# A gated mix of a Fourier layer and a SwiGLU: the gate/up stage written out in one order, and the stream's loads moved to ScalarE

## The chip, the cores and the metric

The kernel runs on one core of a Trainium2 chip. A core has TensorE (PE, matrix products, with PEld for its weight loads), VectorE (DVE), ScalarE (ACT), GpSimd (POOL) and SyncE (SP). Each takes its own instructions strictly in order; they meet only at semaphores. SP, ACT and POOL can also start transfers (DMAs); all transfers of the core share 16 DMA engines. The metric is device time in microseconds (us), lower is better. The kernel before took 740.35 us, the median of three runs (739.05 to 740.51).

## The reference

Sequence length S = 2048, width D = 512, hidden width F = 1376, all in float32. Cut to its core:

```python
a = einsum("bsd,ed->bse", x, dft_hid_re)
b = einsum("bsd,ed->bse", x, dft_hid_im)
y = einsum("ts,bse->bte", dft_seq_re, a) - einsum("ts,bse->bte", dft_seq_im, b)
h = silu(x @ w1) * (x @ w3)
out = h @ w2
g = sigmoid((x * gate_w).sum(-1, keepdims=True))
return g * y + (1 - g) * out
```

## The kernel before, in words

**Precision.** Each float32 operand is split into a high part (a float32r copy made by ScalarE, `nc.scalar.activation` with Copy, L110) and a low part (the difference, `nc.vector.tensor_sub`, L111). A product is three matmuls: high by high, high by low, low by high (`mm3`, L113). Everything TensorE reads has therefore passed through ScalarE and VectorE; the helper `split` does both halves at once.

**Fewer products.** Each 2x2 block product is done with seven products of sums of blocks instead of eight products (a Strassen-Winograd scheme). The sums of blocks, called T1 to T4 on the streamed side, are made on VectorE, the results are collected from TensorE's eight accumulation banks by ScalarE and VectorE.

**Gate/up stage.** Work is cut into 22 items, `ITEMS` (L163): a chunk c of 128 hidden columns times a half g of the sequence. Items 0 to 8 are chunks 0 to 8 for half 0, items 9 to 12 chunks 9 and 10 for both halves, items 13 to 21 chunks 0 to 8 for half 1, whose weights' sums are read back from DRAM (`load_wb`, L207). Item 0 is done with eight plain products. Every other item is `gate_up(n)` (L310), which calls `second(n, ...)` (L285): products into bank X (index 4), Z (5), then `first1(n+3)` (first product of the item three ahead, its own X bank), X (3), Z (2), then `first2(n+3)` (a Y bank), X (6). The document calls them X44, Z55, X33, Z26 and X62. Each accumulates into a bank which ScalarE or VectorE must have read before the next product goes in: u2 is copied from X (L292), u4 from Z (L294), u4 is added to (L297), u2 is added to and multiplied (L299, L300), and the Silu of X (L304) and a multiplication (L305) finish the item; GpSimd stores its result (`store_h`, L278). The Silu is what frees bank X for `first1` of the item after.

**What else is done during the items.** The weights: loads by SP (`load_w`), split of the three plain blocks (`prep_wa`) and sums and split of the other four (`prep_wb`, which also stores them through GpSimd for later). The operand of half 1, XO: four loads, four sums, seven splits at items 3 to 9 (L433 to L439). Four of the six parts of w2, at items 9 to 12 (`prep_w2`, L447): five sums and four splits, and two stores by GpSimd. The sequence-side input x, eight parts A1, seven of them at items 13 to 19 (`make_a`, L461): three sums into a second buffer and two splits each. These are hung into the dictionary `extra` by item and run at the end of `gate_up`.

**Order.** `manual_schedule` for PE and SP (L566) says that these two engines take their instructions as written in the gate/up stage. The order on VectorE, ScalarE and GpSimd there is chosen by a planner from its own estimates of durations; it moves later work between an item's steps. After the gate/up stage all engines are in written order (L575).

**Buffers.** `wide` (L98) takes a 4 KB-per-partition buffer from the list F4, four in the gate/up stage and nine more after it, in memory that the gate/up pools give up. `parts` (L101) takes one for a split pair from ZO, two in the gate/up stage and four after it. Both lists are first in, first out, in program order; an instruction that writes a reused buffer waits for its last reader or store.

**The stream.** 182 steps (`STEPS`, L489) in eight blocks: four "F" blocks (sequence DFT, 28 steps of 12 matmuls each), two "H" (hidden result by w2) and two "Y" (hidden DFT). A block runs through the seven products P1 to P4 of `CHAIN`, each in NQ steps. Step m's `step(m)` does the matmuls, then calls `advance(m)` (L561): `load_c(m + 8)` starts all loads that are due, `sum_c(m + 4)` makes a sum, `split_c(m + 3)` splits the operand for three steps ahead. After the first `split_c` of a B22 block, GpSimd starts an accumulating load that adds B12 into the same buffer (L551): that is operand T3. At the last step of a product its banks are read (ScalarE copies, VectorE adds) and, for four of them, scaled and stored by SP (`spill`, L644). Other work of that time hangs in `todo` by step: the second part of x (`make_a2`, steps 1, 3, ...), the gates (`gates`, a Sigmoid, step 2), the remaining w2 and DFT parts (`late_*`), and the loads of the next block's weights (`load_forms`, SP).

**The seam** between the stages: after item 21, `split_c(0)` and `split_c(1)`, the gate/up pools are closed and the new ones opened in their place, the last part of A1 is made, `advance(-1)` follows, and then the steps begin.

Of the kernel before, what the change touches and what calls it, by code (L numbers as in the profile page):

```python
# [26 lines left out]
K = 9  # L27
XO_AT = 3
W2_AT = (9, 10, 11, 12)
A1_AT = (13, 14, 15, 16, 17, 18, 19)  # L30


@with_exitstack
def fnet_swiglu_gate_kernel(
# [69 lines left out]
    def free(*tiles):  # L104
        for t in tiles:
            _, places, at = HELD.pop(id(t))
            places.append(at)

    def split(hi, lo, src):
        nc.scalar.activation(hi, src, AF.Copy)  # L110
        nc.vector.tensor_sub(lo, src, hi.bitcast(F32))  # L111

# [31 lines left out]
    def splits1(m, t1):  # L144
        split(flat(t1[:, 0, 1:4]), flat(t1[:, 1, 1:4]), m[:, :768])

    def forms1(r, m, t1):
        sums1(r, m, t1)
        splits1(m, t1)

# [37 lines left out]
    def sum_xo(g, k, t):  # L188
        ST[g, k] = t
        nc.vector.tensor_sub(t, *(ST[g, v] for v in SUMS[k]))  # L190

    def split_xo(g, k):
        o = XO[g][:, :, OPS.index(k)]
        split(flat_x(o[:, 0]), flat_x(o[:, 1]), ST[g, k])

# [11 lines left out]
    def load_wb(w):  # L207
        WB[w] = wbp.tile([P, 2, 4, 256], F32R, tag="wb", name=f"wb{w}")
        nc.sync.dma_start(WB[w].bitcast(F32), wbsp[SETS[w]])

    def prep_wa(w, lo=0, hi=3):

        if lo == 0:
            WA[w] = wap.tile([P, 2, 3, 256], F32R, tag="wa", name=f"wa{w}")
        t = WA[w]
        split(t[:, 0, lo:hi].rearrange("p a n -> p (a n)"),
              t[:, 1, lo:hi].rearrange("p a n -> p (a n)"),
              WS[w][:, lo:hi].rearrange("p a n -> p (a n)"))

    def prep_wb(w):  # L220

        r = WS.pop(w)
        u = wup.tile([P, 4, 256], F32, tag="wu", name=f"wu{w}")
# [4 lines left out]
        t = WB[w] = wbp.tile([P, 2, 4, 256], F32R, tag="wb", name=f"wb{w}")  # L228
        split(t[:, 0].rearrange("p a n -> p (a n)"), t[:, 1].rearrange("p a n -> p (a n)"),
              u.rearrange("p a n -> p (a n)"))  # L230
        if w < K:
            nc.gpsimd.dma_start(wbsp[w], t.bitcast(F32))

# [29 lines left out]
    def put_score(n, j, gate):  # L263


        c, g = ITEMS[n]
        if c < NC - 1:
            return
        if j == 0:
            SC[g] = wide(f"sc{g}")  # L270
        t = SC[g].rearrange("p (b n) -> p b n", b=2)
        nc.scalar.activation(t[F % P :, j], gate[F % P :], AF.Copy)
        if j == 1:
            nc.gpsimd.dma_start(gs[2 * g : 2 * g + 2].rearrange("b o n -> o b n"),
                                t[F % P : F % P + 1])
            extra.setdefault(n + 1, []).append(lambda: free(SC[g]))

# [6 lines left out]

    def second(n, between):  # L285
# [4 lines left out]
        u4 = u4p.tile([P, 512], F32, tag="u4", name=f"u4_{n}")  # L290
        prod(x, n, 4, 4, False, True)
        nc.scalar.activation(u2, x, AF.Copy)  # L292
        prod(z, n, 5, 5, True, True)
        nc.scalar.activation(u4, z, AF.Copy)  # L294
        between[0]()
# [5 lines left out]
        between[1]()  # L301
        prod(x, n, 6, 2, False, True)
        put_score(n, 1, x)
        nc.scalar.activation(g1, x, AF.Silu)  # L304
        nc.vector.tensor_mul(g1, g1, u4)  # L305
        store_h(n, h)

    extra = {}

    def gate_up(n):  # L310
        last = NI - 1

        def b0():
            w = WSET[min(n + LOOK, last)] + 1
            if w < len(SETS) and w not in WA and w not in WS:
                load_w(w, 0, 3 if back(w) else 4)
            if n < last and WSET[n + 1] not in WB:
                prep_wb(WSET[n + 1])
            if n + LOOK <= last:
                first1(n + LOOK)  # L320

        def b1():
            if n + LOOK < last and WSET[n + LOOK + 1] not in WA:
                prep_wa(WSET[n + LOOK + 1])
            if n + LOOK <= last:
                first2(n + LOOK)

        if n < last and WSET[n + 1] not in WB and back(WSET[n + 1]):
            load_wb(WSET[n + 1])
        if n + LOOK <= last and WSET[n + LOOK] not in WA:  # L330
            prep_wa(WSET[n + LOOK])
        second(n, (b0, b1))
        for f in extra.get(n, ()):
            f()

# [90 lines left out]
    WS.pop(0)  # L426
    load_w(4)


    def xo_sum(k, b):  # L430
        return lambda: (sum_xo(1, k, ST[1, b]), split_xo(1, k))

    extra[XO_AT - 2] = [lambda k=k: load_xo(1, k) for k in ("B11", "B21", "B12", "B22")]  # L433
    for n, f in enumerate((lambda: split_xo(1, "B11"), lambda: split_xo(1, "B21"),
                           xo_sum("T1", "B11"), xo_sum("T2", "B11"), xo_sum("T3", "B12"),
                           xo_sum("T4", "B21"), lambda: split_xo(1, "B22"))):
        extra[XO_AT + n] = [f]
    for n, k in enumerate((("B12",), ("B11", "B21"), ("B22",))):
        extra[XO_AT + 4 + n].append(lambda k=k: free(*(ST[1, b] for b in k)))  # L439

    W2R = {}

    def load_w2(p):
        W2R[p] = wide(f"w2r{p}")
        nc.sync.dma_start(W2R[p], w2[p])

    def prep_w2(p):  # L447
        r, m, t1, t2 = W2R.pop(p), wide(f"w2m{p}"), parts(f"w2a{p}"), parts(f"w2b{p}")
        forms1(r, m, t1)
        nc.gpsimd.dma_start(w2sp[0][p], t1.bitcast(F32))  # L450
        forms2(r, t2[:, :, :3])
        nc.gpsimd.dma_start(w2sp[1][p], t2[:, :, :3].bitcast(F32))
        free(r, m, t1, t2)

# [5 lines left out]

    def make_a(p, pl=None):  # L461
        A1.append((pl or a1).tile([P, 2, 4, 256], F32R, tag=f"a1_{p}", name=f"a1_{p}"))
        r, m = XR.pop(p), wide(f"xm{p}")
        forms1(r, m, A1[p])
        free(r, m)

    for p, n in enumerate(W2_AT):
        extra.setdefault(n - 1, []).append(lambda p=p: load_w2(p))
        extra.setdefault(n, []).append(lambda p=p: prep_w2(p))
    for p, n in enumerate(A1_AT):  # L470
        extra.setdefault(n - 1, []).append(lambda p=p: load_a(p))
        extra.setdefault(n, []).insert(0, lambda p=p: make_a(p))
    extra.setdefault(NI - 2, []).append(lambda: load_a(NG - 1))
    extra[NI - 1] = [lambda: load_c(2)]

# [78 lines left out]
    def load_c(m):  # L554
        while LOADS and LOADS[0][0] <= m and F4:
            _, blk, k, q = LOADS.pop(0)
            r = RAW[blk, k, q] = wide(f"{k}_{blk}_{q}")
            n = cols(blk, q, k)
            nc.sync.dma_start(r[:, :n], block(blk, "B12" if k == "T3" else k, q)[:, :n])

# [16 lines left out]
    split_c(1)  # L577
    close(*gate_pools)
# [6 lines left out]
    ZO[:0] = [(zo_b, f"zo_{k}") for k in range(2, 4)]  # L585
    make_a(NG - 1, a1b)
    advance(-1)
# [110 lines left out]
    def step(m):  # L698
# [17 lines left out]
        ni = cols(blk, q, form) // 512  # L716
        for r in range(2):
            sl = slice(r * P, (r + 1) * P)
            for n, zn in steps:
                for i in range(ni):  # L720
                    w = ws[2 * n + i]
                    b = slice(i * 512, (i + 1) * 512)
                    mm3(ps[r], w[:, 0, FORM[k], sl], w[:, 1, FORM[k], sl], zn[:, 0, b], zn[:, 1, b],
                        own and n == 0 and i == 0, n == NQ[blk] - 1 and i == ni - 1, not own)
# [136 lines left out]
```

## Time and profile before

One execution was profiled.

| what | value |
|---|---|
| median of three runs | 740.35 us |
| the profiled execution, its own time | 739.09 us |
| its span, first to last instruction | 737.2 us |
| TensorE clock granted, mean | 0.998 |
| ScalarE busy, VectorE busy | 366.2 us (50%), 575.8 us (78%) |
| bytes moved | 186.16 MB, mean 253 GB/s |
| gate/up items 1 to 21 on TensorE | from about 24 to 231 us |
| stream on TensorE | from about 226 to 733 us |

Busy time counts an instruction from its start to its end. Neighbouring instructions of one engine overlap a little, so the sum of durations is more than the busy time. The idle time in brackets behind a row is that of the engine just before it, with the instruction that ended it. A row "L110" or "L111" is the helper `split`, so its tiles tell what is split: zo is an operand of the stream, B a raw block for it, w2a and w2b the splits of w2 with w2r as raw data, xr and xs parts of x, wa and wb weights, xo the operand of the gate/up stage, h, u, s results.

### The profile page before, as it was taken

Reading aid. Unit: us, or ns where it says so; the run is one execution under the profiler, and the core shown is the slowest. Engines: PE = TensorE matmul, PEld = TensorE weight load, DVE = VectorE, ACT = ScalarE, POOL = GpSimd, SP = SyncE. Lnnn points to the kernel's source line nnn. Section 1 sums busy time; section 2 is a strip of 40 time slices with the busy share of each in tenths; the row PEclk is TensorE's granted clock in tenths of the full one; section 3 lists DMA queues with packets and bytes.
Section 4 is the critical chain, followed back from the end, with each engine's and each line's share of the span. In section 5 each row is a group of like instructions: output and inputs, shape, how many; then the busy total and the mean of one; then the engine's idle time right before and its main releaser. Section 6 shows DMA issues by size and latency. Waiting matters only on the chain.

```text
span 737.2 us, 8514 instructions
## 1 busy us (share of the span) xinstructions
PE 714.3 (97%) x3089; PEld 578.1 (78%) x3089; DVE 575.8 (78%) x717; ACT 366.2 (50%) x485; POOL 50.6 (7%) x74
## 2 busy tenths in 40 slices
PE   9999998899999899999999999999999999999997
PEld 6788876688887687888888887887778888887786
DVE  6999885757656887887798759985878596693996
ACT  6775553555433664445454445354535445444361
POOL 0111111110000010001000010001001001000000
PEclk9999999999999999999999999999999999999999
DMA  6665676667769757775967495829999689698862
GB/s 256 231 262 221 261 273 221 247 207 265 266 226 368 286 145 217 280 269 178 271 230 269 140 284 196 338 71 264 353 418 401 149 324 316 162 370 267 282 220 98
DMA packets 49625, 186.16 MB, mean 253 GB/s; under 512 B 5168, under 2 KB 5296, under 8 KB 44976
## 3 DMA queue, kind: packets, MB, share of 16 engines
q1 hardware_dynamic: 39728, 143.15, 53.6%
q0 software_dynamic: 9568, 41.96, 18.8%
q8 instruction: 24, 0.39, 0.2%
q10 hardware_dynamic: 288, 0.52, 0.2%
q14 instruction: 17, 0.14, 0.1%
HBM read 128.45 MB, written 57.16 MB: 252 GB/s over the span
## 4 chain that ended last, share of the span: by engine, by line
PE 45%; DMA 20%; issue 14%; DVE 13%; ACT 6%; SPq 1%; POOL 0%; ACTq 0%; POOLq 0%; DVEq 0%
PE P L115 24%; PE X L115 11%; DMA B<-cc 8%; PE Z L115 5%; DVE zo L111 5%; PE Y L115 3%; ACT zo L110 3%; DMA B<-zsp 3%; DMA B<-hsp 2%; DMA w2sp<-w2b 2%; DVE B L535 2%; DMA xs<-xn 1%; DMA dsp<-late 1%; PE C L115 1%; DMA p5g<-gs 1%
## 5 line engine op out<-in xcount | busy, mean ns | idle before, releaser
L115 PE MATMUL P<-zo,a 128*128 128x512 f32 x1344 | 311.4, 392 | 8.1 <-DVE zo L111 6.1
L115 PEld LDWEIGHTS P<-zo,a 128*128 128x128 f32 x1344 | 252.4, 189 | 66.9 <-DVE zo L111 10.9
L110 ACT ACTIVATE zo<-B 128x1024 fp32r<-128x1024 f32 (+1 forms) x182 | 187.6, 1044 | 214.9 <-DVE B L535 67.4
L111 DVE TENSOR_TENSOR zo<-B,zo 128x1024 fp32r<-128x1024 f32 (+1 forms) x182 | 216.9, 1204 | 88.5 <-ACT zo L110 87.7
L115 PE MATMUL P<-zo,H 128*128 128x512 f32 x468 | 106.5, 389 | 0.2 <-DVE zo L111 0.2
L115 PEld LDWEIGHTS P<-zo,H 128*128 128x128 f32 x468 | 87.8, 188 | 18.8 <-DVE zo L111 0.6
L115 PE MATMUL X<-xo,wb 128*128 128x512 f32 x378 | 93.6, 391 | 3.9 <-ACT h L292 3.9
L535 DVE TENSOR_TENSOR B<-B,B 128x1024 f32<-128x1024 f32 (+1 forms) x78 | 92.9, 1191 | 2.2 <-DMA B<-hsp 2.0
L115 PEld LDWEIGHTS X<-xo,wb 128*128 128x128 f32 x378 | 70.3, 188 | 21.2 <-ACT h L292 6.3
L115 PE MATMUL P<-zo,Y 128*128 128x512 f32 x336 | 77.5, 391 | 1.1 <-DVE zo L111 0.8
L115 PEld LDWEIGHTS P<-zo,Y 128*128 128x128 f32 x336 | 62.8, 188 | 15.6 <-DVE zo L111 2.7
L115 PE MATMUL X<-xo,wa 128*128 128x512 f32 x126 | 32.9, 392 | 4.3 <-ACT h L304 3.5
L115 PE MATMUL Y<-xo,wa 128*128 128x512 f32 x126 | 32.1, 389 | 0.0
L115 PE MATMUL Z<-xo,wb 128*128 128x512 f32 x126 | 32.1, 389 | 0.0
L115 PE MATMUL Z<-xo,wa 128*128 128x512 f32 x126 | 32.0, 389 | 0.0
L115 PEld LDWEIGHTS X<-xo,wa 128*128 128x128 f32 x126 | 23.4, 188 | 10.4 <-ACT h L304 4.4
L115 PEld LDWEIGHTS Z<-xo,wa 128*128 128x128 f32 x126 | 23.7, 188 | 5.0
L115 PEld LDWEIGHTS Z<-xo,wb 128*128 128x128 f32 x126 | 23.6, 188 | 4.9
L115 PEld LDWEIGHTS Y<-xo,wa 128*128 128x128 f32 x126 | 23.6, 188 | 4.9
L297 DVE TENSOR_TENSOR u<-u,X 128x512 f32<-128x512 f32 x21 | 14.4, 685 | 16.6 <-PE X L115 16.5
L551 POOL DMA_DIRECT2D B<-cc x16 | 13.7, 857 | 197.5 <-DVE zo L111 182.8
L110 ACT ACTIVATE wa<-ws 128x768 fp32r<-128x768 f32 (+2 forms) x21 | 17.0, 811 | 20.0 <-PE Z L115 11.7
(107 smaller groups left out, 530.8 us busy)
## 6 DMA issues: line engine op xcount, KB each, us to landing
B<-cc SPq DMA_DIRECT2D x64, 512.0 KB, 6.7
hsp<-h POOLq DMA_DIRECT2D x22, 512.0 KB, 5.2
B<-hsp SPq DMA_DIRECT2D x20, 512.0 KB, 9.6
wbsp<-wb POOLq DMA_DIRECT2D x8, 1024.0 KB, 5.1
wb<-wbsp SPq DMA_DIRECT2D x8, 1024.0 KB, 5.1
B<-cc POOLq DMA_DIRECT2D x16, 512.0 KB, 10.6
B<-zsp SPq DMA_DIRECT2D x16, 512.0 KB, 7.4
H<-w2sp SPq DMA_DIRECT2D x6, 1024.0 KB, 10.6
```

What stands on the lines that cost most here:

```text
L110: nc.scalar.activation(hi, src, AF.Copy)
L111: nc.vector.tensor_sub(lo, src, hi.bitcast(F32))
L115: nc.tensor.matmul(ps, u, v, start=first and n == 0, stop=last and n == 2, skip_group_check=chain)
L297: nc.vector.tensor_add(u4, u4, x)
L535: nc.vector.tensor_add(t, t, RAW[blk, b, q][:, :n])
L551: nc.gpsimd.dma_start(src, block(blk, "B12", q), accum_op=ALU.add)
```

## The change

Seven things are changed, all in the order or the place of work; the products are the same.

- `split` is divided into `high` (ScalarE) and `low` (VectorE), so that the two halves can stand at different places. `prep_wb` is likewise divided into its sums, its high and its low part.
- `gate_up` is written out as one order for all engines: between the seven products of an item stand the reads of its banks, the next weights' work, and three lists of later stages' work, `early` (after X44), `mid` (after X33) and `at_end`. `manual_schedule` now covers all engines from item 1 to the end.
- XO's splits, w2's parts and A1's parts go into these lists in pieces: sums in `early` of item n, high in `mid` of item n, low in `early` of item n+1. w2 is at items 9, 11, 13, 15 (was 9 to 12), A1 at 12, 14, 16 to 20 (was 13 to 19).
- A1 is made in place: three sums that overwrite the raw buffer and one split of all four blocks, in another order of columns (`FORMS`), instead of a second buffer and two splits.
- The two halves' scores share one buffer.
- The first two loads of the stream's first block come at the ends of items 19 and 20 (before, the first three at the end of item 21), and their splits in item 21. The split of weight set 4 stands before item 1.
- The stream's operand loads due from step 0 on are issued by ScalarE, ahead of the split in the same `advance`.

The diff, cut to its core:

```diff
-W2_AT = (9, 10, 11, 12)
-A1_AT = (13, 14, 15, 16, 17, 18, 19)
+W2_AT = (9, 11, 13, 15)
+A1_AT = (12, 14, 16, 17, 18, 19, 20)
...
+    def high(hi, src):
+        nc.scalar.activation(hi, src, AF.Copy)
+
+    def low(hi, lo, src):
+        nc.vector.tensor_sub(lo, src, hi.bitcast(F32))
...
+    def sums1_here(r):
+        a21, a11, a12, a22 = (r[:, i * 256 : (i + 1) * 256] for i in range(4))
+        nc.vector.tensor_sub(a22, a22, a21)
+        for d, v, w in ((a21, a22, a11), (a12, a12, a21)):
+            nc.vector.scalar_tensor_tensor(d, v, -1.0, w, op0=ALU.mult, op1=ALU.subtract)
...
     def gate_up(n):
...
         prod(x, n, 4, 4, False, True)
         nc.scalar.activation(u2, x, AF.Copy)
+        run(early, n)
         prod(z, n, 5, 5, True, True)
         nc.scalar.activation(u4, z, AF.Copy)
+        if nw is not None:
+            sums_wb(nw)
+        if n + LOOK <= last:
+            first1(n + LOOK)
+        if nw is not None:
+            high_wb(nw)
         prod(x, n, 3, 3, False, True)
         nc.vector.tensor_add(u4, u4, x)
+        if nw is not None:
+            low_wb(nw)
+        run(mid, n)
         prod(z, n, 2, 6, False, True)
         nc.vector.tensor_add(u2, u2, z)
         nc.vector.tensor_mul(u2, s1, u2)
+        if wa is not None:
+            WA[wa] = wap.tile([P, 2, 3, 256], F32R, tag="wa", name=f"wa{wa}")
+            parts_a = wa_parts(wa, 0, 3)
+            high(parts_a[0], parts_a[2])
+        if n + LOOK <= last:
+            first2(n + LOOK)
+        if wa is not None:
+            low(*parts_a)
         prod(x, n, 6, 2, False, True)
         put_score(n, 1, x)
         nc.scalar.activation(g1, x, AF.Silu)
         nc.vector.tensor_mul(g1, g1, u4)
         store_h(n, h)
+        run(at_end, n)
...
+    prep_wa(4)
...
+    for n, (k, b) in enumerate((("B11", ""), ("B21", ""), ("T1", "B11"), ("T2", "B11"),
+                                ("T3", "B12"), ("T4", "B21"), ("B22", ""))):
+        if b:
+            do(early, n + 2, lambda k=k, b=b: sum_xo(1, k, ST[1, b]))
+        do(mid, n + 2, lambda k=k: high(*xo_parts(1, k)[::2]))
+        do(early, n + 3, lambda k=k: low(*xo_parts(1, k)))
...
+        if n in W2_AT:
+            p = W2_AT.index(n)
+            do(at_end, n - 1, load_w2, p)
+            do(early, n, sums_w2, p)
+            do(mid, n, high_w2, p)
+            do(early, n + 1, low_w2, p)
+        if n in A1_AT:
+            p = A1_AT.index(n)
+            do(at_end, n - 1, load_a, p)
+            do(early, n, lambda p=p: sums1_here(XR[p]))
+            do(mid, n, high_a, p)
+            do(early, n + 1, low_a, p)
+    do(at_end, NI - 3, lambda: load_c(0))
+    do(at_end, NI - 2, load_a, NG - 1)
+    do(at_end, NI - 2, lambda: load_c(1))
+    do(early, NI - 1, lambda: sums1_here(XR[NG - 1]))
+    do(mid, NI - 1, lambda: split_c(0))
+    do(at_end, NI - 1, lambda: split_c(1))
...
+    FORMS = {"F": FORM | {"P1": 1, "P5": 3, "P6": 0, "P3": 2}, "H": FORM, "Y": FORM}
...
-            nc.sync.dma_start(r[:, :n], block(blk, "B12" if k == "T3" else k, q)[:, :n])
+            (nc.sync if m < LEAD + AHEAD else nc.scalar).dma_start(
+                r[:, :n], block(blk, "B12" if k == "T3" else k, q)[:, :n])
...
-    order = tc.manual_schedule(engines={mybir.EngineType.PE, mybir.EngineType.SP})
-    order.__enter__()
+    ctx.enter_context(tc.manual_schedule())
     for n in range(1, NI):
         gate_up(n)
-        if ITEMS[n] == (NC - 1, 1):
+        if ITEMS[n] == (NC - 1, 0):
             close(xo0_cm)
             a1_cm, a1 = pool("a1", 1, "left")
-
-    order.__exit__(None, None, None)
-    ctx.enter_context(tc.manual_schedule())
-    split_c(0)
-    split_c(1)
```

More of the change, by code (lines that the diff above doesn't have):

```diff
@@ L209, in load_wb, with wa_parts @@
         nc.sync.dma_start(WB[w].bitcast(F32), wbsp[SETS[w]])
+    def wa_parts(w, lo, hi):
+        return (*(flat(WA[w][:, h, lo:hi]) for h in range(2)), flat(WS[w][:, lo:hi]))
     def prep_wa(w, lo=0, hi=3):
@@ L283, in store_h, with run, gate_up @@
         nc.gpsimd.dma_start(o.rearrange("b p n -> p b n"), h.rearrange("p (b n) -> p b n", b=2))
-    def second(n, between):
+    early, mid, at_end = {}, {}, {}
+    def run(work, n):
+        for f in work.get(n, ()):
+            f()
+    def gate_up(n):
+        last = NI - 1
         x, s1 = G.pop(n)
@@ L306, in second @@
         store_h(n, h)
[L308 to L334, printed above, removed]
+        run(at_end, n)
     load_w(0, 0, 1)
@@ L427, in fnet_swiglu_gate_kernel @@
     load_w(4)
[L430 to L439, printed above, removed]
+    prep_wa(4)
@@ new lines, in do @@
+    def do(work, n, f, *a):
+        work.setdefault(n, []).append(lambda: f(*a))
+    for k in ("B11", "B21", "B12", "B22"):
+        do(at_end, 1, load_xo, 1, k)
+    for n, (k, b) in enumerate((("B11", ""), ("B21", ""), ("T1", "B11"), ("T2", "B11"),
[4 more added lines that the diff above has]
+        do(early, n + 3, lambda k=k: low(*xo_parts(1, k)))
@@ L441, in fnet_swiglu_gate_kernel @@
+    for n, k in ((7, "B12"), (7, "B11"), (8, "B21"), (9, "B22")):
+        do(early, n, lambda k=k: free(ST[1, k]))
     W2R = {}
     def load_w2(p):
[L444 to L453, printed above, removed]
+        W2R[p] = [wide(f"w2r{p}")]
+        nc.sync.dma_start(W2R[p][0], w2[p])
@@ new lines, in w2_parts, with sums_w2 @@
+    def w2_parts(p):
+        r, m, t1, t2 = W2R[p]
+        return [*((flat(t1[:, 0, i:j]), flat(t1[:, 1, i:j]), v) for i, j, v in
+                  ((1, 4, m[:, :768]),)),
+                *((flat(t2[:, 0, i:j]), flat(t2[:, 1, i:j]), v) for i, j, v in
+                  ((0, 2, r[:, 512:]), (2, 3, r[:, :256])))]
+    def sums_w2(p):
+        W2R[p] += [wide(f"w2m{p}"), parts(f"w2a{p}"), parts(f"w2b{p}")]
+        r, m, t1, t2 = W2R[p]
+        sums1(r, m, t1)
+        nc.vector.tensor_sub(r[:, :256], r[:, 256:512], r[:, :256])
@@ L455, in fnet_swiglu_gate_kernel, with high_w2, low_w2 @@
+    def high_w2(p):
+        for v in w2_parts(p):
+            high(*v[::2])
+    def low_w2(p):
+        a, b, c = w2_parts(p)
+        low(*a)
+        nc.gpsimd.dma_start(w2sp[0][p], W2R[p][2].bitcast(F32))
+        low(*b)
+        low(*c)
+        nc.gpsimd.dma_start(w2sp[1][p], W2R[p][3][:, :, :3].bitcast(F32))
+        free(*W2R.pop(p))
     A1, A2, XR = [], [], {}
@@ L459, in load_a, with parts_a1, high_a, low_a @@
         nc.sync.dma_start(XR[p], xn[p])
[L461 to L474, printed above, removed]
+    def parts_a1(p):
+        return flat(A1[p][:, 0]), flat(A1[p][:, 1]), XR[p]
+    def high_a(p):
+        A1.append((a1b if p == NG - 1 else a1).tile([P, 2, 4, 256], F32R, tag=f"a1_{p}",
+                                                    name=f"a1_{p}"))
+        high(*parts_a1(p)[::2])
+    def low_a(p):
+        low(*parts_a1(p))
+        free(XR.pop(p))
+    for n in range(NI):
+        if n in W2_AT:
[16 more added lines that the diff above has]
+    do(at_end, NI - 1, lambda: split_c(1))
     CHAIN = (("P1", "B11"), ("P5", "T1"), ("P6", "T2"), ("P3", "B22"),
@@ L716, in step @@
         ni = cols(blk, q, form) // 512
+        f = FORMS[kind][k]
         for r in range(2):
```

73 lines of the change are left out of this document (44 added, 29 removed).

## The prediction

> **What bounds the kernel now.** I read the page's busy shares first, then TensorE's matmuls in order of time, then ScalarE's row in the one stretch where TensorE waits, then the two stretches behind it.
>
> ```profile
> PE 714.3 (97%) x3089; PEld 578.1 (78%) x3089; DVE 575.8 (78%) x717; ACT 366.2 (50%) x485; POOL 50.6 (7%) x74
> ```
>
> TensorE sets the time: the question is only where it stands still. In undisturbed stretches six matmuls start every 1.36 us, 0.2267 us each. The 3078 matmuls behind the eleven of warm-up would take 697.7 us; the first starts at 5.65 and the last ends at 733.3, 727.7 us. So about 30 us are lost. These rows of TensorE in order of time (start, length, matmuls, idle time before them) show most of it:
>
> ```profile
> 109.51 1.65 PE L115 MATMUL X<-xo,wb 128*128 128x512 f32 x6 [1.68 <-ACT h L292]
> 120.39 1.65 PE L115 MATMUL X<-xo,wa 128*128 128x512 f32 x6 [2.43 <-ACT h L304]
> 131.84 1.66 PE L115 MATMUL X<-xo,wa 128*128 128x512 f32 x6 [1.09 <-ACT h L304]
> 145.28 1.65 PE L115 MATMUL X<-xo,wb 128*128 128x512 f32 x6 [1.66 <-ACT h L292]
> ...
> 225.94 0.50 PE L115 MATMUL P<-zo,a 128*128 128x512 f32 x1 [1.16 <-ACT zo L110]
> ...
> 244.67 7.34 PE L115 MATMUL P<-zo,a 128*128 128x512 f32 x24 [1.57 <-DVE zo L111]
> ...
> 289.56 76.50 PE L115 MATMUL P<-zo,a 128*128 128x512 f32 x336 [0.76 <-DVE zo L111]
> ```
>
> I took each row's start minus 0.2267 us for every matmul before it. This running loss is 2.7 us at 106, 11.9 at 147 (so 9.2 in four items), 12.2 at 224, 19.2 at 252 (7.0 at the seam to the stream), 28.9 at 681 and some 30 at the end. Between 147 and 224, and for whole blocks of the stream, it does not grow at all.
>
> The 9.2 us have one kind of cause, which ScalarE's own row shows:
>
> ```profile
> 114.11 0.42 ACT L110 ACTIVATE w2a<-w2r 128x256 fp32r<-128x256 f32 x1 [3.69 <-DMA w2r<-w]
> 118.44 0.63 ACT L110 ACTIVATE w2b<-w2r 128x512 fp32r<-128x512 f32 x1 [3.91 <-DMA w2sp<-w2b]
> 119.09 0.62 ACT L272 ACTIVATE sc<-s 32x512 f32<-32x512 f32 x1
> 119.74 0.60 ACT L304 ACTIVATE h<-X 128x512 f32<-128x512 f32 x1
> ```
>
> ScalarE takes its queue in order. It stood 3.91 us before a split of w2 whose buffer was still being stored; the Silu that frees TensorE's bank X stood behind it, ended at 120.34, and TensorE went on at 120.39. VectorE is not the cause: it is busy 14.0 and 14.1 of the 20 us from 100 and from 120.
>
> **The change, part by part.**
>
> Gate/up on all engines in written order, w2 at items 9, 11, 13, 15. No matmul is added. A steady item is 42 matmuls, 9.52 us. Let t be the time in it: X44 ends at 1.36, Z55 2.72, the next item's first product 4.08, X33 5.44, Z26 6.80, Y 8.16, X62 9.52. Every bank has about 2.7 us between its last matmul and the one that needs it read. I fill the other queues by hand. In a row VectorE's starts lie 0.34 us (256 columns), 0.60 (512), 0.87 (768) and 1.14 (1024) apart (rows from 85.29 to 92.65). An item costs it five 512s, one 768, four 256s and one 1024: 3.0+0.87+1.36+1.14 = 6.4 us. Items with a part of XO add 2.28: 8.7. The fullest, item 12, adds w2's three lows 1.81 and A1's three sums 1.02: 9.2 of 9.52. In that item the Silu of X62 ends at about 2.4 of the next, the bank is needed at 2.72, so 0.3 us are to spare; elsewhere 0.8. w2's store is now issued at about 2 to 4 in item n+1, takes 5.6 (w2a) and 7.4 us (w2b) to land, and the buffers are next written in item n+2 at 2 and 5.4: landed in both cases, by 3 us or more. The loads that ScalarE waits for (w2, xn) are asked for one item ahead, on a slot that VectorE has released by about t=4; they land 4 to 8 us later, before t=2 of the next. So the cause of the 9.2 us is gone. What is late next is item 12's Silu or an xn load; I leave 0.7 for it. Taken: 8.5 us gained, ends 6 and 9.2.
>
> XO's high and low halves lie in neighbouring items, with the same instructions: nothing, hidden by VectorE's 0.9 us to spare in an item; without them a stall of that size per item, at most 1 in all, inside the ends above.
>
> A1 in place: per pair one ACTIVATE of 1058 ns for 418 and 845, one subtraction of 1221 for 420 and 958: 0.2 us less on each engine, eight times, beside TensorE. Zero; behind the gate's end the last pair gives 0.2. The stream's choice of A1's columns follows that layout and costs nothing; one score buffer instead of two frees 4 KB per partition and no time.
>
> The split of wa4 moves into the start-up part. TensorE waits 0.81 us for that very split at 30.13; it can come earlier, or the strict order behind it can delay item 1. Zero, ends -0.8 and +1.
>
> The seam. Let T be the end of the last gate matmul (231.3 before). Two cc blocks are now loaded one and two items earlier, so the 1.32 us at 225.94 go. But only two of them fit in the four wide places; the third goes into a place of the buffer s1 that item 21's multiplication frees at about T, and SP issues in order. Before, six cc loads stood ahead of xs<-xn from about T-2 on; now seven from T on:
>
> ```profile
> 216.15 15.08 SPq L559 DMA_DIRECT2D B<-cc  x9
> 231.51 0.96 SPq L592 DMA_DIRECT2D xs<-xn  x2
> ...
> 240.65 0.95 ACT L110 ACTIVATE a<-xs 128x512 fp32r<-128x512 f32 x2 [4.24 <-DMA xs<-xn]
> ```
>
> At 365 GB/s (slices of 220 to 240) 512 KB take 1.4 us. The third block lands at T+4.3, its two halves end at T+6.7, where step 2 would start at T+5.5: 1.2 us. xs lands at T+1.5+8*1.4 = T+12.7 (before T+9.3), and behind it in ScalarE's queue is the split that step 4 needs: ready at T+16.2 against T+12.3, 3.9 us (before 3.3 by then). After these waits TensorE's clock was halved for 3.4 us (the 24 matmuls in 7.34 us instead of 5.4); the longer wait will do so again, 2 us, of which the next wait takes some. Together 7.8 against 7.0: 0.8 lost, ends -3 (clock not halved) and +4.
>
> The stream's loads. Of 106 loads 9 stay on SP and 97 go to ScalarE. SP's rows for them have a median of 0.43 us (0.33 to 1.18), and ScalarE's own two issues take 0.34. ScalarE pays 42 us where it is busy 238 of 493: 48% becomes 57%. In the stream it waits for PE, VectorE or cc for most of the rest, and its splits run three steps (8.2 us) ahead. What would make it wait is a wide place not yet free: counted in program order, each place a load takes was released four or more steps before (10.9 us) in the F and H blocks, three in Y. Behind each load stand the split of step m+3 and, in every fourth step, the read of a bank. SP in exchange no longer holds loads behind spills, as here, where five cc loads came in one burst:
>
> ```profile
> 295.64 0.33 SPq L654 DMA_DIRECT2D zsp<-zp  x1
> 296.01 2.74 SPq L559 DMA_DIRECT2D B<-cc  x5
> ```
>
> But no stall of the stream comes from a late plain load: those at 289, 366, 444 and 516 follow POOL's accumulating load, B22 plus B12, with 10.6 us to landing, which the change leaves where it is. Zero, ends -3 (fewer loads in a burst ahead of it) and +4 (97 issues of 0.43 us delay some reads; SP's waits of 4.5 us for H<-w2sp, a transfer with none of its tiles, come to ScalarE instead).
>
> Sum: -8.5 +0.8 = -7.7. The profiled execution took 739.09 us for a span of 737.2, and stands 1.26 below the median; the change is carried over: 740.35-7.7 = 732.6.
>
> A rule that speaks against the change: the Trainium skill, "DMA: Bandwidth & Descriptors", section "Issuing engines are not separate DMA queues" with "Queues, rings and completion order", says that all issuers share the same 16 DMA engines, which go round the rows of queues, so another issuer saves issue time only. No run here shows it. By it the accumulating load has two neighbours instead of one, the second rival below.
>
> **The rivals.**
> Better: the accumulating load also lands sooner. For: three cc loads went out at 343.6 to 345.7, right between its issues (344.45 to 355.06); in the new order two come then. 1 us less in each of four F blocks: 728.6.
> Slower: it lands later, because ScalarE's queue moves data beside SP's stores and POOL. Each us of landing beyond 10.6 is a us of TensorE at step 19 of an F block, as there is already a stall there in each. With half of a two-to-three sharing, 10.6/4 = 2.7 us, four times 10.6: 743.2. It decides from 2.3 us a block on, where the 7.7 and another 1.5 are spent. Against: the DMA engines are busy 0.63 to 0.86 in the slices from 340 to 380, and the bytes are the same.
> Smaller: the written order makes its own waits in the gate, one of 0.5 us in each of the eight fullest items: 736.6. For: 0.3 us to spare in item 12; against: 9.2 of 9.52.
> No change: what the gate saves, the seam takes (xs and cc come later by as much, the halved clock longer): 740. Against: both are issued relative to T, not to a fixed time.
>
> **How the numbers follow.** Forecast 0.53 (728.5 to 735.5), better 0.12, smaller 0.17, slower 0.12, no change 0.06. A difference under 0.2% (1.5 us) can't be told here from none. Faster is forecast, better and smaller: 0.82; same 0.06; slower 0.12. The range leaves out most of the slower case and the edges of the better: 725.5 (all four gains at their ends are 724) to 740.
>
> **What would show it.** Right: no waits on h between 106 and 146 and no ACT row waiting for w2sp; gate items of 9.52 us from 35 to 215; a wait of 1 to 4 us within 20 us behind T, with xs as ScalarE's releaser; ACTq rows of about 0.4 us in the stream and no PE wait released by them. Wrong: ScalarE waiting with a load's issue at its head, the accumulating load's median well over 10.6, or gate items over 9.6 us.

## The result and the profile after

The kernel after the change takes 750.22 us (median of 4 runs, 746.76 to 752.82) where the kernel before takes 739.79 (median of 4). The ratio is 1.0138, with a 95% interval of 1.0093 to 1.0183: slower by 1.4%, which is small but clear of the noise, where faster was forecast, and 10 us above the top of the range. The profiled execution took 746.76 us for a span of 744.6. It is the fastest of the four, so the rows below account for 7.7 of the 10.4 us. What the other runs lose beyond that is in no trace.

The busy shares look as before. This line answers the one shown for the kernel before:

```profile
PE 719.0 (97%) x3089; PEld 581.3 (78%) x3089; DVE 579.1 (78%) x709; ACT 366.3 (49%) x477; POOL 50.7 (7%) x74
```

TensorE's rows in order of time, from 100 to 560 us (start, length, matmuls, idle time before them), show what has gone and what has come:

```profile
145.11 1.66 PE L120 MATMUL X<-xo,wa 128*128 128x512 f32 x6 [0.58 <-ACT h L367]
...
210.43 1.66 PE L120 MATMUL X<-xo,wb 128*128 128x512 f32 x6 [1.01 <-ACT h L339]
...
235.70 0.79 PE L120 MATMUL P<-zo,a 128*128 128x512 f32 x1 [2.88 <-ACT zo L109]
237.57 7.94 PE L120 MATMUL P<-zo,a 128*128 128x512 f32 x24 [1.08 <-DVE zo L112]
...
284.44 73.83 PE L120 MATMUL P<-zo,a 128*128 128x512 f32 x323 [0.58 <-DVE zo L112]
359.03 0.50 PE L120 MATMUL P<-zo,a 128*128 128x512 f32 x1 [0.76 <-ACT zo L109]
360.29 2.76 PE L120 MATMUL P<-zo,a 128*128 128x512 f32 x11 [0.76 <-DVE zo L112]
364.17 0.50 PE L120 MATMUL P<-zo,a 128*128 128x512 f32 x1 [1.12 <-ACT zo L109]
...
443.03 0.50 PE L120 MATMUL P<-zo,a 128*128 128x512 f32 x1 [1.33 <-ACT zo L109]
...
523.98 0.49 PE L120 MATMUL P<-zo,a 128*128 128x512 f32 x1 [1.29 <-ACT zo L109]
...
547.12 0.50 PE L120 MATMUL P<-zo,a 128*128 128x512 f32 x1 [1.15 <-ACT zo L109]
```

The four waits of the gate (1.1 to 2.4 us each) are down to two of 0.58 and 1.01. The seam loses about as much as before. But in the stream every F block now stops longer, at its step 18 or 19 or at both (counted from 0), and a new stop stands at 547, at step 110, two steps before the last F block gives way to the first H block.

I count the running loss as in the prediction: the start of a matmul minus 0.2267 us for each matmul before it. All 3078 matmuls are counted, and the kernels are compared at the same matmul, so that a stage begins and ends at the same work in each. Loss in us:

| kernel | gate (to matmul 900) | seam (to 1020) | four F blocks (to 2235) | border F to H (to 2300) | H and Y | sum |
|---|---|---|---|---|---|---|
| before | 12.25 | 7.13 | 6.70 | 1.04 | 2.71 | 29.83 |
| after | 5.02 | 7.92 | 17.23 | 4.12 | 2.97 | 37.26 |
| difference | -7.23 | +0.79 | +10.53 | +3.08 | +0.26 | +7.43 |

The gate gave about what it was to give, the seam took what it was to take, and the stream lost 14 us that the forecast had at zero.

**The F blocks.** The stops follow the accumulating loads. GpSimd issues four of them in each F block, and the split of T3 waits for each. The trace gives for those of the last F block the time from issue to landing, first before, then after:

```profile
DMA to landing us min/median/max: 10.5/11.2/12.1
```
```profile
DMA to landing us min/median/max: 7.7/12.2/15.6
```

The median hardly moves (over all blocks it is 10.6 before and 11.2 after). The fourth load of each block moves most: it took 12.4, 8.7, 10.5 and 10.5 us in the four blocks before, and 13.8, 15.0, 13.6 and 15.6 after. It is the one that TensorE needs last. But it is also issued sooner, because in both kernels GpSimd issues it 0.3 to 0.5 us after the first of the four has landed, and in the last three blocks the first lands sooner than before. So I take the stretch from the first issue to the last landing: the four blocks took 18.5, 19.3, 20.5 and 21.4 us before, and 19.9, 23.2, 21.5 and 23.6 after. The differences, 1.4, 3.9, 1.0 and 2.2, lie beside losses in the same blocks of 1.3, 4.4, 1.1 and 3.8 (the last one holds a stretch of 3.4 us at the halved clock behind the stop).

Why are they later? SP's rows from 495 to 515 in the kernel before show three B21 loads sent in one burst around the issue of the first accumulating load (498.87), and then nothing up to 512.77, where a store and the fourth follow:

```profile
496.76 0.52 SPq L636 DMA_DIRECT2D dsp<-late  x1
497.38 0.56 SPq L624 DMA_DIRECT2D u3p<-dd  x1
497.99 2.08 SPq L559 DMA_DIRECT2D B<-cc  x3
512.77 0.33 SPq L636 DMA_DIRECT2D dsp<-late  x1
513.14 0.49 SPq L559 DMA_DIRECT2D B<-cc  x1
```

After, ScalarE issues those loads one by one beside its splits, all of them behind the first accumulating load (499.14), and SP sends its store 2.6 us sooner (ScalarE's rows, then SP's):

```profile
501.65 0.33 ACTq L636 DMA_DIRECT2D B<-cc  x1
...
504.34 0.33 ACTq L636 DMA_DIRECT2D B<-cc  x1
...
508.20 0.33 ACTq L636 DMA_DIRECT2D B<-cc  x1
512.93 1.06 ACT L109 ACTIVATE zo<-B 128x1024 fp32r<-128x1024 f32 x1 [3.89 <-DMA B<-cc]
512.95 0.34 ACTq L636 DMA_DIRECT2D B<-cc  x1
```
```profile
510.19 0.32 SPq L709 DMA_DIRECT2D dsp<-late  x1
```

From the trace's packets I worked out what share of the 16 DMA engines each queue had in the same block, in pieces of 3 us:

```
before  from us     504   507   510   513   516
  GpSimd           0.65  0.68  0.96  1.05  0.23
  SP               0.40  0.37  0.11  0.00  0.79
after   from us     504   507   510   513   516   519
  GpSimd           0.61  0.75  0.69  0.43  0.44  0.28
  ScalarE          0.38  0.30  0.36  0.25  0.17  0.35
  SP               0.00  0.00  0.00  0.35  0.44  0.08
```

Before, the accumulating loads have one neighbour and then, from 510 to 516, almost none. After, they keep one neighbour to 513, and two from there. The engines are full in both (the shares add up to about 1). So the first accumulating load, with fewer loads ahead of it, lands sooner (7.7 us for 10.6), and the last one later. The sooner landing also brings the store forward: its data is split on ScalarE behind the split that waits for the first accumulating load, and that split began at 506.97 in place of 509.55. The store then runs beside the last accumulating load, where before SP's queue moved nothing from 513 to 516 and most of the store behind that. So by the time of the last landing more has moved beside the accumulating loads. Counted from their first issue, the other queues moved 3.2, 3.7 and 4.0 MB in F blocks 1 to 3 before (the first block is number 0), and 4.1 MB in each of them after.

The Trainium skill, "DMA: Bandwidth & Descriptors", section "Queues, rings and completion order", says that each engine takes a packet from each row that has work, in turn. The trace agrees: a packet of GpSimd's queue took about 0.29 us there, one of ScalarE's 0.15, one of the store 0.32. Taken in turn, GpSimd has 0.29/0.44 = 0.66 with one neighbour and 0.29/0.76 = 0.38 with both; measured are 0.61 to 0.75, and 0.43 and 0.44.

**The border.** TensorE's new stop at step 110 is two waits, 1.15 and 0.76 us, and 3.4 us at the halved clock behind them. ScalarE's rows there show it waiting for a store:

```profile
538.00 1.06 ACT L109 ACTIVATE zo<-B 128x1024 fp32r<-128x1024 f32 x1 [1.23 <-DVE B L612]
538.03 0.33 ACTq L636 DMA_DIRECT2D B<-hsp  x1
546.01 1.06 ACT L109 ACTIVATE zo<-B 128x1024 fp32r<-128x1024 f32 x1 [6.94 <-DMA dsp<-late]
546.03 1.29 ACTq L636 DMA_DIRECT2D B<-hsp  x3
```

The store dsp<-late was issued by SP at 534.92 and landed at 545.93, after 11.0 us, and the split began 0.08 us behind it. It is the split itself that has to wait, and not a load's issue. The late weight parts and the split pairs take their buffers from the same four places of `parts`, first in, first out. Counted in program order, the split for step 110 gets the place that the last late part gave up, and this store reads that place. None of ScalarE's 97 load issues shows a wait for an older transfer, and together they take 35 us. The kernel before has the same wait, and its chain of work shows it (start, length):

```profile
530.90 8.68 DMA dsp<-late
539.66 1.07 ACT zo L110
```

There the store landed after 8.7 us, and step 110 was not held up. SP had sent five of the H block's loads behind the store, in the store's own queue. After the change such loads go through ScalarE's queue, which moved 2.0 MB beside the store until it landed. So the border has the same kind of cause as the F blocks: a transfer that is waited for lands later beside loads from another queue.

### The profile page after: what moved, and what is told of

Same layout as the page of the kernel before. It is cut to its first block, busy times and chain, and to the rows that moved or that the text cites. A ratio compares the mean times of both kernels' runs of the same rounds, so it can differ in the third digit from the quotient of the medians.

```text
span 744.6 us, 8467 instructions
## 1 busy us (share of the span) xinstructions
PE 719.0 (97%) x3089; PEld 581.3 (78%) x3089; DVE 579.1 (78%) x709; ACT 366.3 (49%) x477; POOL 50.7 (7%) x74
## 4 chain that ended last, share of the span: by engine, by line
PE 54%; DMA 19%; issue 15%; DVE 7%; ACT 3%; POOL 1%; SPq 1%; POOLq 0%; ACTq 0%; DVEq 0%
PE P L120 33%; PE X L120 12%; DMA B<-cc 7%; PE Z L120 6%; DVE zo L112 3%; PE Y L120 3%; DMA B<-zsp 3%; DMA p5g<-gs 3%; DMA B<-hsp 3%; ACT zo L109 2%; DMA dsp<-late 1%; PE C L120 1%; DMA hsp<-h 1%; DMA xs_B<-xt 1%; DVE zu L815 1%
## 5 line engine op out<-in xcount | busy, mean ns | idle before, releaser
L120 PE MATMUL P<-zo,a 128*128 128x512 f32 x1344 | 317.4, 396 | 16.7 <-ACT zo L109 9.1
L120 PEld LDWEIGHTS P<-zo,a 128*128 128x128 f32 x1344 | 255.1, 191 | 78.8 <-DVE zo L112 13.6
L120 PEld LDWEIGHTS Z<-xo,wb 128*128 128x128 f32 x126 | 23.6, 188 | 4.9
L120 PEld LDWEIGHTS Y<-xo,wa 128*128 128x128 f32 x126 | 23.6, 188 | 4.9
L309 POOL DMA_DIRECT2D hsp<-h x22 | 16.2, 735 | 134.6 <-DVE h L368 115.1
L284 ACT ACTIVATE s<-s 128x512 f32<-128x512 f32 x21 | 13.2, 631 | 24.0 <-DVE s L282 23.9
## 6 DMA issues: line engine op xcount, KB each, us to landing
B<-cc POOLq DMA_DIRECT2D x16, 512.0 KB, 11.2
```

Of the source, the lines that this page charges most:

```text
L120: nc.tensor.matmul(ps, u, v, start=first and n == 0, stop=last and n == 2, skip_group_check=chain)
L284: nc.scalar.activation(s1, s1, AF.Silu)
L309: nc.gpsimd.dma_start(o.rearrange("b p n -> p b n"), h.rearrange("p (b n) -> p b n", b=2))
```

## The experiments

Three theories were on the table. Q: the loads' row in the DMA queues slows the accumulating loads. S: ScalarE, in order, loses time to the issues and what they wait for. G: the new gate order leaves the stream in a worse state. Each kernel was timed beside the kernel before, and the changes below are differences to that one, to be held against the +10.43 us of the change.

**Loads back on SP.** The changed kernel with one line put back:

```diff
-            (nc.sync if m < LEAD + AHEAD else nc.scalar).dma_start(
+            nc.sync.dma_start(
```

> The changed kernel, but every load of the stream issued by SP again. Three theories. Q (queue rows): the 15 us lost in the stream come from ScalarE's loads being a third row of transfers beside SP's and GpSimd's while the accumulating loads run; with SP alone their landing goes back to 11 us or less and the time to 733 to 735. S (ScalarE in order): the loss comes from the issues' own time and waits in ScalarE's queue; also 733 to 735 here. G (the gate/up order upsets the stream): 748 or more, landings stay at 13 to 15 us for the last of each block.

Measured: 729.82 us against 738.61, -8.8; ratio 0.990 (0.9866 to 0.9935). So everything but this line is worth -8.8 (the forecast had -7.7 for it), and the line costs 19.2 us at the medians. The time is 3 us below what Q and S expected. The fourth accumulating loads of the blocks land after 11.7, 9.5, 11.1 and 11.0 us.

**Only the loads on ScalarE.** The kernel before with that line alone:

```diff
-            nc.sync.dma_start(r[:, :n], block(blk, "B12" if k == "T3" else k, q)[:, :n])
+            (nc.sync if m < LEAD + AHEAD else nc.scalar).dma_start(
+                r[:, :n], block(blk, "B12" if k == "T3" else k, q)[:, :n])
```

> The kernel before, with only this changed: loads due from step 0 on are issued by ScalarE. Q and S: 751 to 755, the last accumulating load of an F block lands 13 us or more after its issue. G: within 2 us of the kernel before.

Measured: 753.26 us, +14.65; ratio 1.0201 (1.0179 to 1.0224). With the old gate order the line does the same, so G falls; these two runs don't tell Q from S. The F blocks lose 18.6 us in place of 6.7, and the last accumulating loads land after 14.0, 14.5, 13.8 and 14.3 us.

**One store out of SP's row.** In F blocks 1 to 3 one late store, of 1 MB, goes through ScalarE's queue, behind its loads. The same bytes are issued, and at nearly the same times (the store goes out 11.5 to 12.2 us behind the first accumulating load, in place of about 11.1), and ScalarE issues more:

```diff
-        nc.sync.dma_start(dst, LATE[i][2 + j][:, :, : 4 - j].bitcast(F32))
+        (nc.scalar if i % 2 and j == 0 else nc.sync).dma_start(
+            dst, LATE[i][2 + j][:, :, : 4 - j].bitcast(F32))
```

> The changed kernel, and the store of a late weight part that falls among the accumulating loads (step 15 of F blocks 1 to 3) is issued by ScalarE too, so that the same bytes stand in one row with the loads instead of two. Q: the accumulating loads' share of the DMA engines rises from 0.4 to about 0.6 in that stretch, their last landing falls to 11 or 12 us in those blocks, time 740 to 745. S: 750 or more, since ScalarE has three more issues and waits. If only the bytes count and not the rows: 750 too, landings unchanged.

Measured: 742.08 us, +3.5; ratio 1.0052 (1.0033 to 1.007): 7 us better than the change. The F blocks lose 8.4 us in place of 17.2. The last landings are 12.1, 11.6 and 13.0 in the three blocks with the edit, and 13.9, as in the changed kernel (13.8), in the one without. From the store's issue to the last landing GpSimd's queue had 0.51 to 0.57 of the DMA engines, in place of 0.43 to 0.47, and until that landing the other queues had moved 3.4, 3.4 and 3.7 MB beside it. More issues on ScalarE and less time: S can't explain the F blocks. The border grew to 7.2 us in this kernel: the store dsp<-late took 10.7 us to land, and 6.8 us at the halved clock lie around the stop.

**B21 loads seven steps earlier.** They stay on ScalarE, and are issued before the accumulating loads:

```diff
+    for blk in range(NTB):
+        NEED[blk] = NEED[blk][:3] + (("B21", 5, 7),)
```

> The changed kernel, with the B21 loads of the F blocks seven steps earlier (steps 5 to 8 instead of 12 to 15), so that ScalarE's row is empty while the accumulating loads run; as many issues as before. Q: last landing 10.5 us or less, time 735 to 738. S: 749 to 752, because the number of ScalarE's issues is the same.

Measured: 733.34 us, -5.3; ratio 0.993 (0.9906 to 0.9953), 15.7 us better than the change with as many issues on ScalarE, and a little below what Q expected. The trace gives for the accumulating loads of the last F block

```profile
DMA to landing us min/median/max: 6.4/6.9/8.1
```

and in F blocks 1 to 3 the other queues move only 1.6, 1.7 and 1.9 MB beside them. TensorE runs through these blocks but for one wait of 1.04 us at 324; what is left is the border (these are its rows from 245 to 534, and ScalarE's row that the last one waits for):

```profile
245.92 77.21 PE L120 MATMUL P<-zo,a 128*128 128x512 f32 x336 [0.44 <-DVE zo L112]
324.17 207.21 PE L120 MATMUL P<-zo,a 128*128 128x512 f32 x911 [1.04 <-DVE zo L112]
533.15 0.49 PE L120 MATMUL P<-zo,a 128*128 128x512 f32 x1 [1.77 <-ACT zo L109]
```
```profile
532.04 1.06 ACT L109 ACTIVATE zo<-B 128x1024 fp32r<-128x1024 f32 x1 [7.29 <-DMA dsp<-late]
```

**Both: loads on SP, B21 early.**

> The changed kernel with all stream loads on SP and the B21 loads of the F blocks seven steps earlier. Q (the accumulating loads are slowed by what shares the DMA engines with them): landings of the accumulating loads 8 us or less in the F blocks, the stalls at their last steps gone (6 us in the run with SP alone), 724 to 726. If those stalls have another cause (VectorE's work at that place): 729 to 731 as with SP alone.

Measured: 725.83 us against 739.62, -13.8; ratio 0.9811 (0.9781 to 0.984). The accumulating loads land after 6.6 to 8.2 us in F blocks 1 to 3, and after up to 9.6 in block 0, where 8 or less was expected. TensorE's rows from 244 to 640 us have no stop at all behind the seam:

```profile
244.75 289.14 PE L120 MATMUL P<-zo,a 128*128 128x512 f32 x1271 [0.53 <-DVE zo L112]
533.72 106.46 PE L120 MATMUL P<-zo,H 128*128 128x512 f32 x468
```

So the stops that the kernel before had in its F blocks were also the accumulating loads' neighbours (the loads that SP had queued just ahead of them), and not VectorE.

**The H block's loads on SP.** B21 early, and only the loads of the first H block moved off ScalarE:

```diff
-            (nc.sync if m < LEAD + AHEAD else nc.scalar).dma_start(
+            (nc.sync if m < LEAD + AHEAD or blk == NTB else nc.scalar).dma_start(
```

> The changed kernel with the B21 loads early, loads on ScalarE, but those of the first H block (due from step 112 on) on SP. Theory C: at the border to H a load's issue on ScalarE waits for the landing of an older transfer that shares no tile with it (a store to dsp, 6.9 us in the changed kernel), and holds the splits behind it, which costs 5 us there; then 728 to 730, 4 to 5 us under the run with B21 early alone, and ScalarE's wait for dsp is gone. If that stall comes from the load of weights on the DMA engines: 732 to 734, no change. Against the run with SP and B21 early it shows what ScalarE's remaining issues cost: 3 us or less.

Measured: 729.65 us against 739.62, -10.0; ratio 0.9862 (0.9837 to 0.9888), 4.7 better than with those loads on ScalarE. The border's loss went from 4.7 us to nothing, which settles that the H block's loads on ScalarE cause it. Theory C named the wrong way, though: ScalarE's wait for dsp is still there, at the same split, only shorter:

```profile
527.44 1.06 ACT L109 ACTIVATE zo<-B 128x1024 fp32r<-128x1024 f32 x1 [1.75 <-DMA dsp<-late]
```

With the H block's loads behind it in SP's queue the store lands 5.8 us after its issue, in place of 11.4. In all ten kernels this split begins 0.08 us behind that landing. The three kernels in which TensorE stops at step 110 are those where the store took 10.7 to 11.4 us; in the other seven it took 5.7 to 8.7. One of these seven is the kernel before with its loads on ScalarE (8.3 us), so loads there do not always bring the stop. Against the kernel with all loads on SP 3.8 us remain, where 3 or less was expected. In the profiles 2.5 more are lost at the seam: there ScalarE's first load goes out beside SP's, xs lands 13.0 us after its issue, and TensorE waits 4.55 us in place of 1.66. How much of this the queue makes is open, since the kernel with B21 early has the same order at the seam and lost only 0.6 more there. The F blocks lose another 1.7.

**Pieces of A1 moved at the seam.** With loads on SP and B21 early, the gates go from step 2 to step 4, and the eight pieces of A1 from steps 1, 3, ... 15 to steps 5, 7, 9, 11, 13, 15, 17, 18:

```diff
-        at(0, 2 * p + 1, make_a2, p)
-    at(0, 2, gates, 0)
+        at(0, (5, 7, 9, 11, 13, 15, 17, 18)[p], make_a2, p)
+    at(0, 4, gates, 0)
```

> As the one before, and the second part of x is made four steps later (steps 5 to 18 instead of 1 to 15), the first gates at step 4 instead of 2, so that ScalarE does not wait for xn at the seam. If that wait and the halved clock behind it are what the seam loses (6 us): 3 to 5 us faster than the one before, 720 to 722, and no halved clock. If the seam is bound by the arrival of the seven cc blocks: within 1 us of the one before.

Measured: 725.0 us, ratio 0.9801 (0.9775 to 0.9826): within the interval of the kernel without the edit, so the expected gain did not come. The seam's loss did fall, from 6.6 us to 0.2. But the first F block lost 8.9 in place of 0.7, with TensorE's rows there

```profile
277.18 0.99 PE L120 MATMUL P<-zo,a 128*128 128x512 f32 x3 [1.53 <-ACT a L109]
280.18 20.02 PE L120 MATMUL P<-zo,a 128*128 128x512 f32 x75 [2.01 <-ACT a L109]
```

and 6.8 us of halved clock behind them. The pieces had been pushed among the block's own T splits.

**The same, the pieces earlier.** Steps 4, 5, 7, 8, 9, 10, 12, 13:

> Against e6 only the steps of A1's eight pieces in the stream's first block change: 4, 5, 7, 8, 9, 10, 12, 13 for 5 to 18, so that none lies among the splits of the block's T products (steps 13 to 19) or beside the accumulating load. If the 1.53 and 2.01 us of TensorE's waits on ScalarE's a at 277 to 280 us in e6, and the 6.8 us of halved clock behind them, came from the pieces at steps 15 to 18, both go: 5 to 6 us less than e6, 719 to 721 us, with the seam's loss still near 0.7 us. If instead pieces at steps 4 and 5 bring the seam's wait for xs back, the seam loses 3 to 6 us again and the time is that of the kernel with the early B21 loads alone, 725 to 726 us. If the waits at 277 to 280 us had another cause, they stay and the time is 725 us with the seam unchanged.

Measured: 721.65 us against 740.13, -18.5; ratio 0.9749 (0.9726 to 0.9773). The waits on a at 277 to 280 are gone. The time lies just above the 719 to 721 expected: the seam loses 2.15 us, where near 0.7 was expected, and the first F block 2.5. TensorE still waits there for 0.57, 0.76 and 0.55 us between 240 and 247.

This version beats both kernels: it keeps the new gate order, leaves the stream's loads on SP, loads B21 ahead of the accumulating loads and spreads A1's rest. The running loss of these kernels by stage, as in the first table:

| kernel | gate | seam | F blocks | border | H and Y | sum |
|---|---|---|---|---|---|---|
| loads on SP | 4.60 | 6.58 | 6.65 | 0.00 | 2.39 | 20.22 |
| before, loads on ScalarE | 12.05 | 8.94 | 18.63 | 0.66 | 2.51 | 42.79 |
| store through ScalarE | 5.37 | 8.11 | 8.43 | 7.20 | 3.78 | 32.89 |
| B21 early | 5.62 | 7.20 | 2.48 | 4.70 | 1.49 | 21.49 |
| on SP, B21 early | 5.13 | 6.62 | 0.71 | 0.00 | 1.97 | 14.43 |
| B21 early, H block on SP | 4.64 | 9.10 | 2.36 | 0.00 | 3.06 | 19.16 |
| A1's pieces moved | 4.74 | 0.24 | 8.86 | 0.00 | 2.78 | 16.61 |
| A1's pieces earlier | 5.00 | 2.15 | 2.92 | 0.06 | 2.98 | 13.11 |

## Why the prediction was wrong

- **The gate, -8.5 (ends -6 and -9.2): right.** Measured -7.23. No ACT row from 106 to 146 waits for w2sp any more. In place of the 0.7 us left for what is late next, 2.3 are lost between 106 and 215, of which TensorE's two rows on h carry 1.6.
- **XO in pieces, A1 in place, wa4 at zero: right** as far as a difference can be seen. At 106 us, behind wa4's place and most of XO's pieces, the two kernels have lost 2.69 and 2.68. A1's pieces come later and lie inside the 2.3 us named above.
- **The seam, 7.8 against 7.0: right in size, in part by luck.** Measured 7.92 against 7.13. xs landed 11.9 us behind the last gate matmul (12.7 forecast), and the waits are 2.88 and 1.08. The 1.2 us at step 2 for the third block did not come. The clock was halved for 6.8 us, not 3.4: the granted clock is 0.66 in the ten microseconds from 235. The wait that did not come and the longer halved clock about cancel.
- **"The stream's loads ... Zero, ends -3 and +4": this step failed.** Measured +13.9 in the profile (F blocks 10.53, border 3.08, H and Y 0.26), +14.65 at the medians with that line alone and 19.2 as the difference of the changed kernel with and without it. The upper end was taken from ScalarE's issues and waits. Of the two things it named, the 97 issues of 0.43 us delayed nothing that shows: the kernel with B21 early has as many and 2.5 us of loss in its F blocks. The other, that waits of SP for a foreign transfer come to ScalarE, did not show: no load issue waits for an older transfer. The border's 3 us come from a transfer that the sum did not look at, the store dsp<-late: it landed after 11.0 us in place of 8.7, and the split that writes the buffer it reads was held up. What failed, then, is the step from "no stall of the stream comes from a late plain load" to zero. The moved loads were not late themselves: they made transfers late that TensorE was already waiting for, or nearly.
- **"The accumulating load ... which the change leaves where it is" was the sentence behind the zero.** GpSimd's issues did stay, but what moves beside them did not. The text weighed the burst of loads that SP sent ahead of them only as a burden ("fewer loads in a burst ahead of it"). The burst was also over by the time that the last accumulating load ran. Tied to ScalarE's steps, the same loads spread over the whole window, and the store moved into its end. The sign named for being wrong, a median well over 10.6, could not have told it: the median is 11.2, while the fourth loads took up to 15.6.
- **The slower rival had the mechanism and nearly the size.** It said 2.7 us a block, 10.6 in all; the F blocks lost 10.53 more. That the two agree so closely is luck: the blocks lost 1.3, 4.4, 1.1 and 3.8, and part of the last is the halved clock. It was given 0.12 because "the DMA engines are busy 0.63 to 0.86 in the slices from 340 to 380, and the bytes are the same". That reason was read from slices of 18 us. In the stretch of the accumulating loads themselves the engines were full already before the change (the columns are busy time by engine, then granted clock, DMA share, GB/s):

```profile
344.00:350.00 6.00, 6.00 (x28) 4.98 (x27) 2.49 (x3) 3.54 (x5) 2.15 (x3) 1.00 1.04 317
350.00:362.00 12.00, 12.00 (x54) 9.94 (x53) 6.63 (x9) 4.83 (x6) 1.32 (x2) 1.00 1.05 247
```

With the engines full, the turn decides who lands first. The same bytes are issued, but what counts is how many of them move before the last accumulating load lands, and that changed (3.2 to 4.0 MB in blocks 1 to 3 before, 4.1 after). With the rival taken at its 10.6 us and the seam and gate as forecast, the time would have come to 743.2, 3.6 below the profiled execution. The border's 3.1 are most of that; the smaller gain in the gate (1.3) and the profiled execution's place below the median (1.26) cancel. The slower median of 750.22 holds another 3.5 us that no trace shows.

- **The rule named beside it** spoke the right way. The part of "Issuing engines are not separate DMA queues" in the Trainium skill's "DMA: Bandwidth & Descriptors" that all issuers end at the same engines is what the packet shares show. Its other half, that a second issuer only saves time on the sequencer, does not hold here: the kernel before lost 14.65 us by it, with the same transfers.

## What to carry to other kernels

Before loads move to another engine's queue, find the transfer that a stop of the bounding engine already follows, and ask in its own few microseconds, not in a slice of the page, whether the DMA engines are full and which transfers will now stand beside it; its last landing counts, not the median. A load that is tied to the steps of a busy engine goes out later and more spread than from a queue that runs ahead. Where a transfer is on the path, issuing its neighbours well ahead of it helps whoever issues them: in the F blocks it took the loss from 17.2 to 2.5 us with the loads on ScalarE and from 6.7 to 0.7 with them on SP, while moving the loads back to SP alone took it from 17.2 to 6.7. And where an engine waits for a transfer that seems to have nothing to do with its work, follow the lists of buffers in program order before calling the wait foreign: here the store read the buffer that the split was to write.

## What was not expected of the hardware

- In the F blocks of the kernels before and after, an accumulating load of 512 KB took 5.6 to 15.6 us to land, by what moved beside it. With the B21 loads out of their way the four of the last F block took 6.4 to 8.1.
- GpSimd issued the fourth accumulating load of a block only 0.3 to 0.5 us after the first had landed, in all eight F blocks of these two kernels. What holds it back was not found.
- TensorE's clock was halved after short waits: for 3.4 us behind waits of 0.31 and 1.57 us in the kernel before, and for 6.8 us behind one of 2.88 in the kernel after. The Trainium skill, "TensorE: Matmul & The Clock Gate", "Part 1: The HAM clock gate", ties the lower clock to an idle window of about 3.4 us; here less was enough. At the seam of the kernel after, waits of 2.88 and 1.08 us so made most of a loss of 7.92. Waits of 1.29 and 0.77 us at 525 and of 1.15 and 0.76 at 548 were also followed by 3.4 us at half the clock; waits of 1.33 and 0.76 at 444 were not.
- After waits of 1.66 and 1.57 us at the seam of the kernel with loads on SP and B21 early the clock was not halved at all. What decides between these cases was not found.
